# Longer key turns in a planner's prices, a plan searched again under random delays, and weight fetches that wait for copied columns

## The chip, the cores and the metric

One core of a Trainium2 chip. The metric is the device time of one execution in microseconds (us); lower is better. The kernel before took 822.94 us in the median of three runs (822.06 to 825.85).

## The reference, cut to what matters

```
q, k, v: (4, 8, 1152, 64)   w_in: (512, 2048)   w_out: (2048, 512)
q_pool = mean of pairs of rows of q                    # 576 queries per head
scores = q_pool @ k.T / 8;  attn = softmax(scores)     # 576 x 1152 per head
x = (attn @ v), heads side by side                     # 2304 tokens x 512
h = x @ w_in;  g = log(1 + exp(h));  out = g @ w_out   # 2304 x 2048, 2304 x 512
```

Inputs are float32. The kernel splits most operands into a high and a low float16 part and adds three float16 products for each float32 one.

## The kernel before, in words

**Work.** The attention is 16 units, each one batch and two heads. A unit loads its keys and queries (`raw`), measures and splits them (`kcat`, `qcat`, `qlow`), and has the parts transposed by DMA: keys at L819 (`kT <- kcat`), queries at L847 (`qA <- qcat`) and L857. Unit 0 is turned on TensorE instead; unit 1's low query rows are too. Then come the row maxima (`maxima`), scores, exponentials, the product with `v`, and the division by the row sums. The feed-forward layer runs on blocks of tokens. Six blocks are plain (`feed_forward`). The last 1024 tokens go through `seven` in four steps n = 0 to 3 of 256 tokens: a 2 x 2 scheme with seven products in place of eight, first with `w_in` (`product`, in two halves q = 0 and 1, results in buffers `p` and `g`), then with `w_out` (`down`, results in `acc`). It needs sums of weight blocks, which `terms` computes earlier and leaves in DRAM as `td`.

**Fetching the sums.** `fetch_sums(1, ...)` (L1615) brings six pieces of 512 KB for `w_out` into the buffers of `kT`, `kB` and `v`, which are free after the last attention unit. `fetch_first(1, ...)` (L1671) brings two more over a part of `w2`. In the plan each of the six has one of the products of step 0 ahead of it, and the last two have the first products of `down`. These are entries in the planner's list of dependencies and no more: in the program the DMA waits only for what its data need, which is that the buffer is free.

**Order.** All work is a list of tasks, each with ways to run it (engine, price in ns), dependencies, a priority and buffers that it takes and gives back. `Sched.run` (L142) simulates the engines with these prices and writes the instructions of each engine in the order in which the simulation starts them. That order is fixed in the program: each engine, and SP, whose queue issues all DMAs, works in order and waits at each instruction for what its data need. A DMA's price is a pair: time on SP's queue, and time on the wire. Two tables steer it, by kind of task and index: `NUDGE` adds to priorities, and `LEAN` adds to the price of an engine where there is a choice.

The lines that the change touches: L734 (first key load), L819 (key turn), L1417 and L1426 (fetches), L1507 (`held`, the four buffers of one half), L1555 (price of softplus), L1615 (deps of the six fetches), L1617 and L1667 to L1675 (order around `down`).

Of the kernel before, what the change touches and what calls it, by code (L numbers as in the profile page):

```python
# [21 lines left out]
    "prep": [3, 5.75, -3.75, -1.5, -55.75, 25.25, 2, 13.25, 3, -6.5, -78.25, -6.75, -19.25, 0, -13.75, 0],  # L22
    "value": [-1.25, 0.25, 4.75, -3.5, -3.75, 0, 0, -38, -4.25, 0.25, 8.5, 3.25, -12.25, 11.5, 0, 13.25],
    "most": [0, 0, 1.25, 10.25, 8.75, -108.25, 0.5, 0.25, 10, -10.75, -8.25, -2, 3.25, 21, 0.75, 3.75],
    "shift": [-5.75, -8.25, -7.75, -0.25, -13.75, -43.5, 7, 7.5, -72.75, -18.75, -104.5, 2.5, -29.75, -1.5,
        0, 1.25],
    "attend": [-11.75, -4, -2.5, 11.5, -6.75, 0, -14, 0.5, -2, -6, -3.5, 6.25, 11, -45.25, 2.25, 0],
    "product": [1.75, 3.5, -31, 120.75, 50.25, -20.5, 10.5, 3.75, 1, 22, -51, 0, 17.5, 19.75, -10.75, 24.75],
    "close": [0, -4.5, -5.75, 0, 31.5, 23, -18, 0, -49.5, -3.75, -58.75, 5, -17.75, 0.5, -3.25, 0],
    "win": [0, -24.5, -5.75, -9.75, 1.75, 2, -3.75, -3],  # L30
    "wout": [-15, -15.25, 5.75, -10.75, -12.25, 28.75, 12, -11.25, -87.25, -24.25, 1, 4.75, 0, -5.25, 2.25,
        -63.25],
    "wparts": [47.75, 0, 38.75, 3.25, 0, -7, -4.25, 0.75, 6.25, -20.5, 0, 0, -0, -40.75, 0, 0],
    "split": [-2.5, 36.75, -3.5, -25.75, 8.5, 5.5, 2.5, 38.5],
    "up": [-5, 1.5, 0.75, 8.5, 0, -0.75, -20.75, -3.25],
    "down": [-9.5, 7.25, 4.25, 15, 0.5, 0, 17.75, -6.75],
    "terms": [1.5, 11.5, 2.5, 12.25, -13.25, 9.75, 0.75, 0.75, -37, 16.25, -6.5, 8.75, -1.5, -9.5, 9, 14],
    "vsplit": [1.75, 0, 16.5, 11],
    "vup": [23.75, 35.75, 28.5, -6, -22.75, -1, -4.25, 0],
    "vdown": [52.25, 1.5, 9.75, -3.75],  # L40
# [4 lines left out]
        "prep": [-50, 150, 0, -100, -0, -600, 4600, 150, 0, 200, -600, -400, -800, -350, 1350, -50],  # L45
        "value": [-250, -550, 250, 1350, 700, -1500, 0, 1200, -250, 350, 500, -750, -300, 2550, -1300, 0],
        "most": [1250, 0, -850, -750, -100, -350, 0, 1000, 0, 50, -950, -500, -950, -200, 0, -350],
        "shift": [0, -50, -50, -1200, 0, -0, 350, 900, -50, -1700, 3300, -1050, 650, 0, 450, 1200],
        "attend": [-250, 0, -1000, 0, -2650, -700, -50, 0, 0, -850, 4250, 2950, 0, 0, -250, 350],
        "product": [-250, 0, -950, -1050, 7600, 0, 450, -0, -50, -5050, -1250, -1400, 850, 250, -7500, 900],  # L50
        "close": [0, 0, 0, 1000, 4500, -6050, 3100, -50, -800, 750, -150, -4100, -1700, 1600, -200, -3200],
        "win": [150, 1600, -250, -200, -1800, 0, 1150, -100],
        "wout": [50, 0, -4350, 350, -50, 2150, -1600, 150, 750, 1400, -750, -450, 200, -2250, 0, -150],
        "wparts": [4100, -500, -100, -200, -1100, 1300, 900, -3000, 500, 200, -1800, 0, 200, 450, -650, 1200],
        "split": [-100, 0, 300, 1050, -5350, 0, 0, -1300],
        "up": [1400, 200, 1250, 600, -550, 1350, -950, 50],
        "down": [-1300, 0, 450, 400, -1150, 1200, -50, -300],
        "terms": [-50, -50, 1000, -350, 1750, -200, 0, -250, 400, -250, -200, 100, 600, -250, 1050, 0],
        "vsplit": [-200, -350, 50, 1800],
        "vup": [0, 2150, 0, 950, 0, -200, -500, 150],  # L60
        "vdown": [500, 950, -400, 50],
    },
    "ACT": {
        "prep": [0, 50, 0, 7650, -3300, 1050, -800, -2350, 450, -800, 3650, -500, -300, 250, -400, -5500],
        "value": [1250, -3550, 300, -1950, 350, -900, -350, 300, 950, -2450, 0, -1150, 0, 200, -450, 0],
        "most": [1250, -3150, 250, -1150, 0, 0, 300, 50, 1550, 0, 100, -100, 0, 850, -250, 550],
        "shift": [-50, -300, 3850, 0, 5650, -450, 250, -100, 1650, -6250, -2350, 300, 1850, -1350, -600, 0],
        "attend": [3000, 1100, 850, 0, 0, -250, 900, -1100, -400, 0, -1350, -0, -850, -1350, 350, 1600],
        "product": [550, -1000, -800, 700, 4400, -300, -1550, -200, -1650, -600, 0, -0, 100, 1200, 0, 1550],
        "close": [-200, 100, -2200, 1400, 1700, 550, 700, 0, -250, 5100, 1500, 0, 550, -300, 4500, -400],  # L70
        "win": [-3850, -2100, -1300, 0, -6100, -350, 0, -4950],
        "wout": [-200, 0, 0, 0, 1700, 0, -600, -300, 100, 250, 50, 1250, 1500, 1450, -4100, -250],
        "wparts": [-650, -1500, 2700, 850, -200, -4350, -2250, 250, 350, 1550, -2700, -1350, 400, -1900,
            -300, 600],
        "split": [2000, -6050, 0, -3400, -950, -750, -750, 450],
        "up": [200, -50, -3500, 0, 400, 0, -750, 550],
        "down": [-3900, -2450, 0, -550, -1800, -150, 650, -700],
        "terms": [150, -800, -1700, -650, 950, 7200, 200, 100, -1400, 3950, 1550, 0, 500, -4650, 0, -1250],
        "vsplit": [-2700, 5400, 0, -600],
        "vup": [-50, 200, -1400, -1350, 250, 0, -1500, 250],  # L80
        "vdown": [0, -1050, 1150, -900],
# [174 lines left out]
def act(n, psum=0, ap=0):  # L256
    return n * 0.833 + (168.0 if psum else 200.0) + 92.0 * ap
# [11 lines left out]
def tile_attention_softplus_ffn(  # L269
# [9 lines left out]
    nc = tc.nc  # L279
# [181 lines left out]
    def load(fn, queue, wire, deps, prio, take):  # L461
        return task([("DMA", queue + 95.0, fn, wire)], deps, prio, take=take)
# [242 lines left out]
    def prepare(u):  # L705
# [15 lines left out]
        def low():  # L721
# [12 lines left out]
            400.0, 2340., units[u - 1].raw_free if u > 2 else [units[0].kB_done] if u == 2 else [], prio - 6.0, [r])  # L734
# [725 lines left out]
    v_x_free, fives = [], [[], []]  # L1460
# [4 lines left out]
    def seven(n):  # L1465
# [36 lines left out]
        split_done = {}  # L1502
        for q in range(2):
# [3 lines left out]
            held = [Hold(ring, 4) for _ in range(4)]  # L1507
# [38 lines left out]
            def soft(o, i, m, deps, p, take=(), give=()):  # L1546
# [8 lines left out]
                return task([("ACT", 4 * act(128 * m, m == 1, m > 1), fn, "softplus")], deps + exps[NU - 1][-5:] + [f1], p,  # L1555
# [33 lines left out]
            g12 = soft(lambda Q=Q: Q(1), lambda Q=Q: Q(1), 1, [c12], at["P3"] + 1)  # L1589
            prio += 7.5  # L1590
# [26 lines left out]
        o1, o2 = Hold(acc_r), Hold(acc_r)  # L1617
# [56 lines left out]
        c1 = scaled(at(o2, 0), lambda: region("P1"), [ps["P1"]], prio + 2, [o2, o1], [pairs[0]])  # L1674
        u2 = plus(at(o1, 1), "P6", at(o2, 0), [ps["P6"], c1])  # L1675
# [84 lines left out]
```

## Time and profile before

| | |
|---|---|
| median of 3 runs | 822.94 us (822.06 to 825.85) |
| the profiled execution | 822.63 us |
| its span, first to last instruction | 820.8 us |
| TensorE busy | 779.7 us (95%) |
| VectorE, ScalarE, GpSimd busy | 680.9, 556.6, 227.4 us |
| mean granted TensorE clock | 0.995 |

PE is TensorE's matmuls, PEld its weight loads, DVE VectorE, ACT ScalarE, POOL GpSimd, SPq the queue of SyncE that issues the DMAs. L819 is line 819 of the kernel before. A row of the windows gives a stretch from the span's start, its length, the busy time of each engine with its instructions, the granted clock, the DMA engines' busy share and GB/s. The profiled execution is 1.8 us longer than its span and 0.3 us below the median.

### The profile page before, as it was taken

The numbers are of one execution on the slowest core, as the hardware profiler recorded it, in microseconds if no ns is written. First come the engines' busy times: TensorE is split into PE (matmuls) and PEld (weight loads), VectorE is DVE, ScalarE is ACT, GpSimd is POOL, SyncE is SP. The second block draws the span as 40 slices with busy tenths as digits, with TensorE's granted clock in tenths as the row PEclk, the third lists the DMA queues.
The fourth block names the chain that finished last, engine by engine and source line by source line (L and its number), as shares of the span: only waits on it lengthen the run. The fifth ranks groups of instructions, "written<-read, shape, count | busy, mean of one in ns | idle before, by whom it ended". The sixth has DMA issues, their size and how long they took to land.

```text
span 820.8 us, 29645 instructions
## 1 busy us (share of the span) xinstructions
PE 779.7 (95%) x12626; PEld 610.0 (74%) x12626; DVE 680.9 (83%) x1475; ACT 556.6 (68%) x968; POOL 227.4 (28%) x213
## 2 busy tenths in 40 slices
PE   4899999999999999989999999999999799999997
PEld 2556656679765976767976688775677799999995
DVE  7978999899979979878999997987573499889862
ACT  6999899898966567678766676867772457333521
POOL 1000001200443223548459862021722110012100
PEclk9999999999999999999999999999999999999999
DMA  8768969968055475652745354465253600000230
GB/s 272 208 157 219 211 183 218 166 181 226 17 115 159 72 145 139 170 86 81 163 126 104 101 116 125 132 126 76 64 167 72 220 4 4 29 30 3 64 96 15
DMA packets 152400, 99.75 MB, mean 122 GB/s; under 512 B 95180, under 2 KB 132044, under 8 KB 152268
## 3 DMA queue, kind: packets, MB, share of 16 engines
q1 hardware_dynamic: 152268, 97.86, 47.8%
q8 instruction: 99, 1.62, 0.9%
q14 instruction: 33, 0.27, 0.1%
HBM read 60.29 MB, written 15.28 MB: 92 GB/s over the span
## 4 chain that ended last, share of the span: by engine, by line
PE 67%; DVE 16%; DMA 4%; issue 4%; ACT 4%; SPq 2%; POOL 2%; DVEq 0%; ACTq 0%; POOLq 0%
PE s L380 28%; PE m L380 23%; PE pv L1128 13%; DVE g L918 2%; DMA qA<-qcat 1%; PE pv L1144 1%; ACT p L1117 1%; DMA raw<-in_q_dram 1%; DMA raw<-in_k_dram 1%; POOL acc L457 1%; PE m L1199 1%; DVE g L1543 1%; PE pv L380 1%; DVE g L457 1%; DVE raw L372 1%
## 5 line engine op out<-in xcount | busy, mean ns | idle before, releaser
L1117 ACT ACTIVATE p<-s,cols 128x512 f32<-128x512 f32 (+1 forms) x288 | 210.2, 742 | 50.5 <-PE s L380 33.7
L1128 PE MATMUL pv<-p,v 128*64 128x320 f32 (+1 forms) x1152 | 188.2, 414 | 0.9 <-DVE rinv L369 0.9
L380 PE MATMUL s<-qA,kT 128*64 128x320 f16 (+1 forms) x1152 | 158.6, 288 | 4.9 <-ACT p L1117 4.5
L380 PE MATMUL s<-qB,kB 66*64 66x320 f16 (+1 forms) x1152 | 159.1, 288 | 0.0
L457 POOL TENSOR_TENSOR acc<-acc,p 128x512 f32<-128x512 f32 (+1 forms) x76 | 116.4, 1531 | 73.9 <-ACT p L1117 58.0
L380 PEld LDWEIGHTS <-w1h 128*64 128x64 f16 x2560 | 114.6, 110 | 5.9 <-issue 3.4
L918 DVE CUSTOM_DVE_ANT_0 g<-m,g 128x512 f32<-128x512 f32 x142 | 96.2, 682 | 25.5 <-ACT g L914 13.5
L380 PE MATMUL m<-w,gh 128*64 128x512 f16 (+1 forms) x808 | 108.0, 349 | 0.7 <-DVE acc L372 0.6
L380 PEld LDWEIGHTS <-kT 128*64 128x64 f16 x1152 | 80.4, 111 | 31.2 <-issue 11.9
L1128 PEld LDWEIGHTS pv<-p,v 128*64 128x64 f32 x1152 | 78.6, 137 | 29.9 <-issue 11.1
L380 PE MATMUL s<-xo,w1h 128*64 128x256 f16 (+1 forms) x1792 | 100.3, 250 | 0.2 <-DVE xo L372 0.2
L914 ACT ACTIVATE g<-m 128x512 f32<-128x512 f32 x142 | 83.8, 598 | 20.4 <-PE m L380 19.5
L380 PEld LDWEIGHTS <-kB 66*64 66x64 f16 x1152 | 75.6, 110 | 19.1 <-issue 5.2
L380 PEld LDWEIGHTS <-qA 128*64 128x64 f16 x1040 | 62.1, 110 | 34.3 <-issue 12.9
L380 PEld LDWEIGHTS <-gh 128*64 128x64 f16 x944 | 59.7, 110 | 22.0 <-issue 1.6
L380 PE MATMUL m<-kT,qA 128*64 128x512 f16 (+2 forms) x588 | 72.2, 301 | 3.3 <-DVE nm L918 1.9
L457 DVE TENSOR_TENSOR acc<-acc,p 128x512 f32<-128x512 f32 (+1 forms) x92 | 71.4, 776 | 4.0 <-ACT p L1117 3.3
L380 PE MATMUL m<-w,gl 128*64 128x512 f16 (+1 forms) x456 | 72.1, 340 | 0.6 <-DVE acc L372 0.6
L380 PEld LDWEIGHTS <-w1l 128*64 128x64 f16 x1280 | 64.7, 110 | 3.6 <-issue 3.6
L380 PE MATMUL m<-kD,qA 128*64 128x512 f16 x284 | 57.7, 386 | 6.7 <-DMA qA<-qcat 4.9
L380 PE MATMUL s<-xo,w1l 128*64 128x256 f16 (+1 forms) x896 | 63.4, 250 | 0.2 <-issue 0.2
L1362 ACT ACTIVATE g<-s,blk 128x512 f32<-128x512 f32 (+1 forms) x48 | 29.4, 616 | 48.4 <-PE s L380 44.1
(279 smaller groups left out, 1412.3 us busy)
## 6 DMA issues: line engine op xcount, KB each, us to landing
raw<-in_k_dram SPq DMA_DIRECT2D x16, 576.0 KB
v<-in_v_dram SPq DMA_DIRECT2D x16, 576.0 KB
raw<-in_q_dram SPq DMA_DIRECT2D x64, 128.0 KB
raw<-in_moe_w_out_dram SPq DMA_DIRECT2D x16, 512.0 KB
td<-to SPq DMA_DIRECT2D x32, 256.0 KB
kB<-kT SPq DMA_DIRECT2D x32, 144.0 KB
gl<-in_moe_w_in_dram SPq DMA_DIRECT2D x4, 1024.0 KB
gh<-in_moe_w_in_dram SPq DMA_DIRECT2D x4, 1024.0 KB
```

Source lines behind the costliest of these rows:

```text
L372: nc.vector.scalar_tensor_tensor(out=out_, in0=in0, scalar=s, in1=in1, op0=op0, op1=op1)
L380: nc.tensor.matmul(out=out_[c:e], lhsT=lhsT[:, c:e], rhs=rhs, start=start, stop=stop, tile_position=(0, at + c))
L457: e.tensor_tensor(out=o, in0=a, in1=b, op=op)
L914: r = task([("ACT", act(512, 1), lambda: nc.scalar.activation(out=rest.item, in_=more.item, func=ACTF.Relu))], [y], prio, take=[rest], giv ...
L918: parts.append(task([("DVE", dve(512), lambda: nc.vector.tensor_tensor_reduce(out=rest.item, in0=most.item, in1=rest.item, scale=1.0, scal ...
L1117: nc.scalar.activation(out=pt.item[:, :, 0:n], in_=s.item[:, :, 0:n], func=ACTF.Exp, scale=x.sc)
L1128: nc.tensor.matmul(out=pv.item[h * 64:(h + 1) * 64, 0:n], lhsT=x.v.item[:, h, kt], rhs=pt.item[:, h, 0:n], start=(kt == 0), stop=(kt == KT ...
L1144: nc.tensor.matmul(out=pv.item[g:g + 32, 512 - n // 2:512], lhsT=ones[:, 0:32], rhs=pt.item[:, h, a * n // 2:(a + 1) * n // 2], start=Fals ...
L1199: nc.tensor.matmul(out=ps.item[g:g + 32, 512 - n // 2:512], lhsT=ones[:, 0:32], rhs=acc.item[:, h, a * n // 2:(a + 1) * n // 2], start=Tru ...
L1362: x = task([("ACT", act(N, 1, 1), lambda: nc.scalar.activation(out=gs.item[:, 0:N], in_=ps.item[:, 0, 0:N], func=ACTF.Softplus, scale=ih[: ...
L1543: return task([("DVE", dve(512), lambda: nc.vector.tensor_tensor(out=o(), in0=bank_(), in1=i(), op=ALU.add))], deps, p, give=list(give))
```

## The change

- Both tables, `NUDGE` and `LEAN`, hold other numbers throughout, so the order on every engine's queue is another.
- A key turn (L819) is priced at 2750 ns on the queue and 1700 on the wire, before 2095 and 1150. The first key load is priced at 1150 ns, before 400 + 95 as the others (the 95 is added to both). A softplus of four pieces is priced at 1190 or 1650 ns, before 1098 or 2021.
- In step 0 of `seven` GpSimd copies one column of a result into the first column of each buffer that a fetch will overwrite. The fetch then has to wait in the program too: the six for the results u3, c21, c12 of half 0 and then of half 1, the two others for c1 and u2 of `down`. `held`, `o1` and `o2` are given back after these copies as well.
- c1 and u2 of `down` are listed before its third product, and the first product of one step's `down` follows the last of the step before in the plan.

The core of the diff, with the tables left out:

```diff
@@ prepare
-            400.0, 2340., units[u - 1].raw_free if u > 2 else ...
+            400.0 if u else 1150.0, 2340., units[u - 1].raw_free if u > 2 else ...
...
-            x.k_done = [task([("DMA", 2095.0, lambda: nc.sync.dma_start_transpose(
-                out=x.kT.item, in_=cat.item.rearrange("p t d -> p (t d)")), 1150.0, 1700.0)], parts, prio,
+            x.k_done = [task([("DMA", 2750.0, lambda: nc.sync.dma_start_transpose(
+                out=x.kT.item, in_=cat.item.rearrange("p t d -> p (t d)")), 1700.0, 1700.0)], parts, prio,
@@ fetch_sums(w, homes, deps, prio, gates=None)
             h = Hold(homes[2 * (t - 1) + hl])
+            first, take = deps[2 * (t - 1) + hl], [h]
+            if gates:
+                y, i, held = gates[2 * (t - 1) + hl]
+                first, take = [task([("POOL", 150.0, lambda h=h, i=i: nc.gpsimd.tensor_copy(flat(h)[:, 0:1], i()), "port")],
+                                    first + [y], prio, take=take, give=held)], []
@@ fetch_first(w, deps, prio, gate=None)
+            first = deps[hl]
+            if gate:
+                first = [task([("POOL", 150.0, lambda hl=hl: nc.gpsimd.tensor_copy(late["part"](w, hl)[:, 0, 0:1], gate[hl][1]()), "port")],
+                              first + [gate[hl][0], saved[w, hl]], prio, give=[gate[hl][2]])]
@@ seven
-            held = [Hold(ring, 4) for _ in range(4)]
+            held = [Hold(ring, 7 if n == 0 else 4) for _ in range(4)]
...
-                return task([("ACT", 4 * act(128 * m, m == 1, m > 1), fn, "softplus")], ...
+                return task([("ACT", 1190.0 if m == 1 else 1650.0, fn, "softplus")], ...
...
+            if n == 0:
+                for y, i in ((u3, 3), (c21, 2), (c12, 1)):
+                    gates.append((y, lambda i=i, Q=Q: Q(i)[:, 0:1], held))
...
-            fetch_sums(1, [kT_r] * 2 + [kB_r] * 2 + [v_r] * 2, [late["ended"] + [v_x_free[i]] for i in (5, 6, 8, 9, 11, 12)], when)
+            fetch_sums(1, [kT_r] * 2 + [kB_r] * 2 + [v_r] * 2, [late["ended"]] * 6, when, gates)
...
+            if name == "P2":
+                c1 = scaled(at(o2, 0), lambda: region("P1"), [ps["P1"]], prio + 2, [o2, o1], [pairs[0]])
+                u2 = plus(at(o1, 1), "P6", at(o2, 0), [ps["P6"], c1])
             if n == 0 and name == "P5":
-                fetch_first(1, [downs + [ps["P1"]], downs + [ps["P6"]]], prio + 5.0)
+                fetch_first(1, [downs] * 2, prio + 5.0, ((c1, lambda: wide(o2, 0)[:, 0:1], o2), (u2, lambda: wide(o1, 1)[:, 0:1], o1)))
-            ps[name] = down(name, [ps[DOWN[i - 1]]] if i % 2 else [], [] if i % 2 else [pairs[i // 2]])
+            ps[name] = down(name, [ps[DOWN[i - 1]]] if i % 2 else last_down[-1:], [] if i % 2 else [pairs[i // 2]])
+        last_down[:] = [ps["P3"]]
```

## Rows read from the trace of the kernel before

**Rows 1.** Busy time on the page, and its row of TensorE's code loads (packets, MB, share).

```profile
PE 779.7 (95%) x12626; PEld 610.0 (74%) x12626; DVE 680.9 (83%) x1475; ACT 556.6 (68%) x968; POOL 227.4 (28%) x213
q8 instruction: 99, 1.62, 0.9%
```

**Rows 2.** Windows: start, stages of the span, end.

```profile
0.00:20.00 20.00, 8.33 (x96) 5.12 (x96) 15.21 (x32) 13.13 (x23) 2.90 (x9) 1.00 0.83 268
20.00:180.00 160.00, 151.12 (x2073) 98.53 (x2075) 144.06 (x381) 144.99 (x251) 13.48 (x20) 1.00 0.80 198
180.00:640.00 460.00, 450.49 (x6023) 342.42 (x6019) 386.00 (x826) 324.58 (x535) 193.60 (x166) 0.99 0.49 116
640.00:660.00 20.00, 15.64 (x554) 15.34 (x551) 11.12 (x18) 8.42 (x21) 2.31 (x3) 1.00 0.63 213
660.00:800.00 140.00, 138.01 (x3622) 136.77 (x3618) 120.22 (x211) 62.42 (x134) 15.14 (x15) 1.00 0.12 33
```

**Rows 3.** Waits of PE: total us, times, longest.

```profile
PE m L380 <- ACT kcat L547: 6.4, 1, 6.4
PE m L380 <- DMA qA<-qcat: 4.9, 2, 2.6
PE s L380 <- ACT p L1117: 4.5, 9, 1.4
PE m L380 <- issue: 4.4, 2, 3.1
```

**Rows 4.** Windows around those waits for issue.

```profile
643.60:646.20 2.60, 2.43 (x87) 2.29 (x82) 2.34 (x5) 1.47 (x5) 0.74 (x2) 1.00 1.03 413
646.10:647.20 1.10, 0.00 (x0) 0.00 (x0) 0.98 (x2) 0.00 (x0) 0.00 (x0) 1.00 1.00 406
647.28:654.14 6.86, 3.76 (x128) 3.60 (x127) 2.67 (x4) 0.92 (x3) 0.00 (x0) 1.00 0.82 243
```

**Rows 5.** Timeline of PE there (start, length, idle before and releaser).

```profile
647.29 0.33 PE L380 MATMUL m<-xo,w1h 128*64 128x128 f16 x5 [1.27 <-issue]
654.15 0.24 PE L380 MATMUL m<-xo,w1l 128*64 128x128 f16 x1 [3.10 <-issue]
```

**Rows 6.** Timeline of SP's queue: first and last fetches of `w_out` sums.

```profile
638.62 0.98 SPq L1422 DMA_DIRECT2D kB<-td  x1
641.08 1.10 SPq L1422 DMA_DIRECT2D v<-td  x2
642.22 5.05 SPq L1399 DMA_DIRECT2D w<-td  x2
```

**Rows 7.** Chain of waits, near 364 and 568 us.

```profile
360.66 2.92 SPq L819
363.64 4.98 DMA qA<-qcat
568.40 7.22 DMA qA<-qcat
```

**Rows 8.** Windows at those two places.

```profile
366.00:368.00 2.00, 0.36 (x8) 0.09 (x2) 1.36 (x1) 0.84 (x2) 1.08 (x1) 1.00 1.54 107
368.00:374.00 6.00, 5.34 (x40) 3.22 (x42) 2.10 (x6) 3.91 (x8) 3.06 (x5) 0.72 0.77 209
572.00:576.00 4.00, 0.97 (x9) 0.34 (x7) 0.83 (x3) 0.27 (x1) 0.26 (x2) 1.00 1.14 128
576.00:582.00 6.00, 6.00 (x60) 4.22 (x58) 2.54 (x8) 4.22 (x8) 4.49 (x5) 0.72 0.55 156
```

**Rows 9.** Key turns on SP's queue (min/median/max ns, first and last start).

```profile
L819 SPq DMA_TRANSPOSE kT<-kcat x15: 2374/2924/3652, 27.9 to 565.7; - x15
```

**Rows 10.** Timelines: results and first users of fetches, POOL's smallest operation.

```profile
650.45 0.69 DVE L1543 TENSOR_TENSOR p<-s,p 128x512 f32<-128x512 f32 x1 [3.34 <-PE s L380]
670.99 0.68 DVE L1543 TENSOR_TENSOR g<-m,g 128x512 f32<-128x512 f32 x1
674.04 1.50 PE L380 MATMUL m<-kT,gl 128*64 128x256 f16 x24
691.32 1.50 PE L380 MATMUL m<-v,gh 128*64 128x256 f16 x24
659.18 0.48 POOL L428 TENSOR_SCALAR xo<-xT,blk 128x256 f16<-128x256 f32 x1 [14.79 <-PE s L380]
665.55 0.33 PE L380 MATMUL s<-xo,w1h 128*64 128x128 f16 x4
```

More of the change, by code (lines that the diff above doesn't have):

```diff
@@ L21 @@
 NUDGE = {
[L22 to L40, printed above, removed]
+    "prep": [-8, 1.75, -7.75, -55.25, -67.5, 21.5, 3.25, 24.5, -2.5, -3.5, -132.75, -6, -26, 13.25, -5.25,
+        0.5],
+    "value": [7.5, 5.5, 2.25, 8, -9.5, 0.75, 6.75, -49, 0.75, -22.25, -6.25, -3.75, -36, 23.75, -45.5, 11.75],
@@ new lines @@
+    "most": [-3.75, 0.75, 1.75, 22.5, 0.5, -170.75, 0, -7.5, -1, -20.75, -56.5, 0.25, -4.25, -5.75, -3.5,
+        -0.75],
+    "shift": [-20.75, -42.25, -37.5, -2, -0, -134.5, -2.25, -5.75, -218.5, -94.25, 0, 5.75, 6.75, -44.75, -8,
+        25.5],
+    "attend": [-10.75, -4.5, 0, 2.25, 0.5, 1, -14.5, 0.75, 1, -22, 0, -10.5, -0.5, -10, 0, 8.75],
+    "product": [-1.25, 6, -10.75, 126.75, 83.25, -37.25, 10.75, 76, 1.25, 24.5, 0, -10, 21, 0.75, 23, 1.5],
+    "close": [1.25, -4, 2.25, -5.25, 48.5, 24.5, -17.25, 4.25, 5.5, -39.25, -42.25, 0, 10, 12, 23.25, 18.75],
@@ new lines @@
+    "win": [-1.25, -126.25, -9.75, -14.5, -0.5, 13.75, -12, 24],
+    "wout": [-7.5, 57, -4, 0, 0.75, 8, 5, 7.75, 0, 26.25, -0, -0.25, 2.5, 1, 25.5, -43.75],
+    "wparts": [24.75, -11, 0, 18.25, -11.75, 0, 16.75, 0, -23, 0, 2, -5.75, -62, -12, 14.5, 0],
+    "split": [-34.75, 32.5, -6, 17.5, -14.25, 58.75, -22.5, 12.25],
+    "up": [2.75, -0.75, -0.5, 0, 16.75, -15.25, 27, -15.25],
+    "down": [-16.5, 96.5, -3.5, 35.75, 20.5, 0, -12.5, -6],
+    "terms": [-0.75, 5.25, 5.5, -2.75, 0.5, 9.75, 8.5, 6.75, -21.5, 4, -30, -61, 1, 8, -7.75, -12],
@@ L41 @@
+    "vsplit": [-25, 1.5, -0.75, 9.25],
+    "vup": [0, -4, -5, 0, -24.75, 0.75, -3, 27.5],
+    "vdown": [5.25, 23, 34, 82.5],
 }
@@ L44 @@
     "POOL": {
[L45 to L61, printed above, removed]
+        "prep": [-150, 850, -500, -550, 6600, 0, 0, 0, 5950, 0, -200, 0, 3400, 650, 0, -600],
+        "value": [-50, 2050, 1700, 1050, 150, -200, -750, -350, -2850, 200, 1900, 700, 200, 0, -600, 2200],
@@ new lines @@
+        "most": [800, 550, -1650, 3650, -1450, 50, -550, 150, 100, -750, -650, 300, -1100, 1650, -100, 950],
+        "shift": [550, 400, -1550, 1650, -4850, -150, -1000, 0, 50, -4950, 50, 100, -50, 0, 1000, -750],
+        "attend": [0, 300, 1150, 0, 550, 1800, -450, 50, 0, 1400, 400, -1000, 1350, -700, 0, -0],
+        "product": [350, 0, 450, 0, 5450, 100, 0, 300, -5650, -3800, 50, 0, 600, 0, -1850, 0],
+        "close": [2700, 0, 0, 4050, -1650, -7000, 1250, 0, -2800, -5450, -1200, -4300, -3000, -6700, 900, -0],
@@ new lines @@
+        "win": [-1150, 400, -1500, -200, 700, 750, -150, -1500],
+        "wout": [150, -650, -1600, -400, 1350, 950, -400, -750, 0, -1050, -300, -1250, 650, 1350, 1750, -400],
+        "wparts": [2500, -50, 1000, -0, -5100, -150, -50, -4650, 0, 350, -500, 100, 2050, -650, 1750, 1500],
+        "split": [-6500, 4050, 2650, -1150, 900, 400, -900, -3500],
+        "up": [400, 100, 900, -750, -1250, 100, 4350, -1300],
+        "down": [0, -1650, 400, 750, -2450, 1050, 50, 150],
+        "terms": [1650, 50, 550, -400, 0, 0, -150, 250, 0, 0, 900, 0, -850, 600, 1250, 850],
@@ L62 @@
+        "vsplit": [-0, 1150, -300, -150],
+        "vup": [-500, 2250, -250, -2400, -900, 250, -300, -900],
+        "vdown": [-1100, -100, 150, 1800],
     },
     "ACT": {
[L64 to L81, printed above, removed]
+        "prep": [0, -250, -800, 8500, -8700, 950, 200, -2000, 2200, -2400, 8350, 650, -4400, 850, 0, -1000],
@@ new lines @@
+        "value": [-3750, 300, -800, 0, 0, -1650, 1200, -600, -1500, 1950, 2250, 1000, -3800, 0, 0, -1100],
+        "most": [1250, 1700, 600, 450, -450, -5500, 50, -2200, 2900, 0, -300, 7400, -450, -150, 1050, 0],
+        "shift": [0, -2850, 3000, 650, 0, 0, -150, 3700, -200, -0, -350, 0, 350, -1900, 900, 0],
+        "attend": [1000, -4550, -700, 100, 0, 0, -100, -1550, 1300, 1300, 1500, 0, 1650, -750, 400, -350],
+        "product": [-2700, 1300, -50, -0, 50, 0, 150, -1100, 300, 250, 1650, -2150, -50, 550, 2150, -2550],
@@ new lines @@
+        "close": [0, 400, -8650, 10400, 6400, 50, 4200, 350, -950, 1400, -850, -1400, -2100, 2750, -1350,
+            1750],
+        "win": [-3200, -2050, -550, 150, 800, 0, 1350, -9350],
+        "wout": [0, 450, -150, 1950, 0, -350, 150, -400, -2200, 0, -5100, 750, -100, -100, 200, 2800],
+        "wparts": [-850, -3250, -1000, 0, -550, -6350, 0, 0, -3650, 2200, -50, -150, 450, -3050, -450, 550],
+        "split": [-500, -350, 1250, 0, 350, 250, 0, 400],
+        "up": [0, -100, 1400, -3600, -400, -300, 100, 1650],
@@ L82 @@
+        "down": [0, 100, 3150, 0, 2850, -150, 1650, 250],
+        "terms": [300, -1700, -550, -950, 0, -1550, 550, 400, 200, 10650, -4850, -150, -6250, -2200, 4750,
+            1150],
+        "vsplit": [-650, 0, 0, 600],
+        "vup": [-850, -1950, -1300, -1200, -850, 0, -550, 1900],
+        "vdown": [0, -1550, 1650, -250],
     },
@@ L733, in prepare @@
             in_=k[b, 2 * p:2 * p + 2].rearrange("h (p t) d -> p h t d", t=KT)),
-            400.0, 2340., units[u - 1].raw_free if u > 2 else [units[0].kB_done] if u == 2 else [], prio - 6.0, [r])
+            400.0 if u else 1150.0, 2340., units[u - 1].raw_free if u > 2 else [units[0].kB_done] if u == 2 else [], prio - 6.0, [r])
         qr, qc = Hold(raw_r, 2), Hold(qcat_r)
@@ L1415, in spaced, with fetch_sums @@
         return [[tasks[i * len(tasks) // n]] for i in range(n)]
-    def fetch_sums(w, homes, deps, prio):
+    def fetch_sums(w, homes, deps, prio, gates=None):
         flat = late["flat"]
@@ L1421, in fetch_sums, with fetch_first @@
                 h = Hold(homes[2 * (t - 1) + hl])
+                first, take = deps[2 * (t - 1) + hl], [h]
[3 more added lines that the diff above has]
+                                        first + [y], prio, take=take, give=held)], []
                 x = load(lambda h=h, w=w, t=t, hl=hl: nc.sync.dma_start(out=flat(h), in_=td[w][t][:, hl]),
-                         390.0, 2000.0, deps[2 * (t - 1) + hl] + term_done[w], prio, [h])
+                         390.0, 2000.0, first + term_done[w], prio, take)
                 late[w, t, hl] = (x, lambda h=h: flat(h))
-    def fetch_first(w, deps, prio):
+    def fetch_first(w, deps, prio, gate=None):
         for hl in range(2):
@@ L1429, in fetch @@
                 late["moved"](late["part"](w, hl), td[w][0][:, hl], w, False)
-            x = load(fetch, 390.0 * (2 - w), 2000.0, deps[hl] + term_done[w] + [saved[w, hl]], prio, [])
+            first = deps[hl]
+            if gate:
+                first = [task([("POOL", 150.0, lambda hl=hl: nc.gpsimd.tensor_copy(late["part"](w, hl)[:, 0, 0:1], gate[hl][1]()), "port")],
+                              first + [gate[hl][0], saved[w, hl]], prio, give=[gate[hl][2]])]
+            x = load(fetch, 390.0 * (2 - w), 2000.0, first + term_done[w] + [saved[w, hl]], prio, [])
             late[w, 0, hl] = (x, None)
@@ L1459, in tile_attention_softplus_ffn @@
     HL = ((0, 0), (0, 1), (1, 0))
-    v_x_free, fives = [], [[], []]
+    v_x_free, fives, last_down = [], [[], []], []
     def flat2(t):
@@ L1502, in seven @@
         split_done = {}
+        gates = []
         for q in range(2):
@@ L1553, in fn @@
                         nc.scalar.activation(out=a, in_=c, func=ACTF.Softplus, scale=ih[:, 4 * q + jj:4 * q + jj + 1])
-                return task([("ACT", 4 * act(128 * m, m == 1, m > 1), fn, "softplus")], deps + exps[NU - 1][-5:] + [f1], p,
+                return task([("ACT", 1190.0 if m == 1 else 1650.0, fn, "softplus")], deps + exps[NU - 1][-5:] + [f1], p,
                             take=list(take), give=list(give))
@@ L1614, in seven @@
             mark("vsplit", 1)
-            fetch_sums(1, [kT_r] * 2 + [kB_r] * 2 + [v_r] * 2, [late["ended"] + [v_x_free[i]] for i in (5, 6, 8, 9, 11, 12)], when)
+            fetch_sums(1, [kT_r] * 2 + [kB_r] * 2 + [v_r] * 2, [late["ended"]] * 6, when, gates)
         mark("vdown", n)
-        o1, o2 = Hold(acc_r), Hold(acc_r)
+        o1, o2 = Hold(acc_r, 2 if n == 0 else 1), Hold(acc_r, 2 if n == 0 else 1)
         prio = when + 14.0
@@ L1668, in seven @@
         for i, name in enumerate(DOWN):
+            if name == "P2":
+                c1 = scaled(at(o2, 0), lambda: region("P1"), [ps["P1"]], prio + 2, [o2, o1], [pairs[0]])
+                u2 = plus(at(o1, 1), "P6", at(o2, 0), [ps["P6"], c1])
             if n == 0 and name == "P5":
                 mark("vsplit", 1)
-                fetch_first(1, [downs + [ps["P1"]], downs + [ps["P6"]]], prio + 5.0)
+                fetch_first(1, [downs] * 2, prio + 5.0, ((c1, lambda: wide(o2, 0)[:, 0:1], o2), (u2, lambda: wide(o1, 1)[:, 0:1], o1)))
                 mark("vdown", n)
-            ps[name] = down(name, [ps[DOWN[i - 1]]] if i % 2 else [], [] if i % 2 else [pairs[i // 2]])
-        c1 = scaled(at(o2, 0), lambda: region("P1"), [ps["P1"]], prio + 2, [o2, o1], [pairs[0]])
-        u2 = plus(at(o1, 1), "P6", at(o2, 0), [ps["P6"], c1])
+            ps[name] = down(name, [ps[DOWN[i - 1]]] if i % 2 else last_down[-1:], [] if i % 2 else [pairs[i // 2]])
+        last_down[:] = [ps["P3"]]
         c11 = plus(at(o1, 0), "P2", at(o2, 0), [ps["P2"], c1])
```

## The prediction

> **What bounds the kernel now.** I read the page's busy times first: TensorE is busy 779.7 of 820.8 us [rows 1]. What can be won without changing its work is its 41 us of idle time and whatever its clock loses. So the second view is the windows, by stages, for where it idles [rows 2]: 11.7 us before 20 us, 8.9 in the next 160, where VectorE and ScalarE are both busy for 144 to 145 of 160 us, 9.5 in the 460 us from 180, 4.4 in only 20 us from 640, 2.0 in the 140 us after that, and the rest at the end. The third is the waits of PE [rows 3]. Two entries there are long, late in the span and single: 4.4 us in two waits for "issue", which is time in which PE waits for nothing that the profile shows, and 4.9 us in two waits for a query transpose. The reader is to see that the change speaks to these two and that the largest wait, 6.4 us at the start, is the first unit's own chain, of which it alters only the price of one load.
>
> **The wait for issue.** Rows 4 show the DMA engines full at 406 to 413 GB/s when PE stops for the first time. What fills them is on SP's queue: from 638.6 us the six fetches and the two others leave one behind the other, the last two taking 5.05 us to issue because nothing moves ahead of them [rows 6]. Eight pieces of 512 KB are 4.2 MB, at 410 GB/s some 10.2 us. They leave together since the program lets them go as soon as the buffers are free, whatever the plan says. Why should PE care, when it needs none of them for 30 us [rows 10]? Between its two stops [rows 5] it ran 128 matmuls and 127 or 128 weight loads [rows 4], that is 256 instructions; and the page counts 99 code loads of 1.62 MB together [rows 1], 16.4 KB each, for 2 x 12626 = 25252 instructions, 255 to a load. PE therefore stops where one load's worth of code ends. I read this as code that comes late because its transfers share the full DMA engines.
>
> The Trainium skill speaks against this: "Runtime: NRT & Kernel Launch", section "Instruction fetch mechanics", says that the sequencer fetches the next block of code over its own DMA queue while it runs the present one, and that crossing a block is mostly hidden. The trace agrees on the block (256 instructions between stops) and not on the hiding (1.27 and 3.10 us [rows 5]). By the rule the fetches would not be the cause and spreading them would give nothing; that is a rival below.
>
> **The change part by part.**
>
> *The gated fetches.* Removed: the burst, and with it 1.27 + 3.10 = 4.4 us of PE. Each fetch now waits for a result. In the trace of before these results lie from 651.1 us (u3 of half 0, 650.45 + 0.69) to 671.7 (c12 of half 1) [rows 10], so six fetches of 1.3 us each (512 KB at 410 GB/s) are spread over 20 us, and the two of `down` come later still. A single fetch holds the DMA engines for less than the 3.6 us in which PE works through one load of code (256 instructions in 3.76 us [rows 4]), so I expect no stop from one. What is late next? The first product that reads the `kT` fetches starts at 674.0, 22 us or more after their gates, and the one that reads the `v` fetches at 691.3, 19.6 us after the last gate [rows 10]. If one more stop came in place of two, it would be 1.3 to 3.1 us. After 660 us VectorE is busy for 120 of 140 us [rows 2], and during the stop it idled too (11.1 busy of 20), so it can take the earlier start. I count the whole 4.4.
>
> *The copies.* Eight copies of one column on GpSimd. No row shows one. From below they are nothing, as GpSimd is busy for 2.3 us of the 20 from 640 and 15.1 of the 140 after [rows 2]; they remove no work, so they can't gain by themselves. From above each is the smallest operation shown there, 0.48 us [rows 10], 3.8 us together on an idle engine. I take nothing, nearest to what an idle engine charges. What a copy does is wait: behind it on GpSimd stands a split of the next step's tokens (`xo`, 659.18), and behind each gated fetch on SP's queue the next fetch and later the output stores. The stores have 100 us to go; the split does not, and makes the price of a mishap: placed behind the copy that waits for c12 of half 1, it would move from 659.2 to 671.7, and the products at 665.55 [rows 10] with it, by up to 12.5 us less what other products fill. The planner knows this dependency, so I leave it in the upper bound.
>
> *The key turns.* The trace has 2374 to 3652 ns on the queue, 2924 in the middle [rows 9]; the plan counted 2095, and 2750 after. Per turn the plan moves what follows by 655 ns on the queue and 550 on the wire, 1.2 us together. Twice this hits PE: at 360.66 and 565.7 a key turn stands ahead of a query turn on the queue, and PE waits 2.3 and 2.6 us for the query turn [rows 3, 7]. Behind each stands a stretch of lower clock: the granted clock is 0.72 over 368 to 374 and again over 576 to 582, after PE was busy for 0.36 of 2 and 0.97 of 4 us [rows 8]; 0.28 x 6 = 1.7 us each. So the two stops cost 4.9 + 3.4 = 8.3 us. The new prices show the planner 1.2 of the 2.3 to 2.6 us of each, about half. From both sides: nothing, if the new order only moves the stop, and 8.3, if the order puts the query turn first. I take half, 4.1.
>
> *The new order.* Everything else on the queues moves, at prices that are the old ones. PE's idle time from 20 to 640 us is 8.9 + 9.5 = 18.4 us, 13.5 without the two stops. Half of that, 6.7 us, is as much as I would credit to another order; the other side is new stops at (4.9 + 3.4) / 2 = 4.15 us each. A search under random delays should prefer orders with slack ahead of the DMAs, which speaks for fewer such stops, and pay for it in nominal time. I take nothing. The new softplus prices (1190 for 1098, 1650 for 2021) change no instruction by themselves. The order between steps of `down` and the later return of `held`, `o1` and `o2` cost nothing while PE has products at hand; without that cover one product of 1.3 us.
>
> Sum on the profiled execution: 822.63 - 4.4 - 4.1 = 814.1; the median is 0.3 above that execution, so 814.4 us.
>
> **The rivals.**
>
> *Only the fetches count.* The burst goes and the new order is worth what the old one was: 822.9 - 4.4 = 818.5 us. For it: the old tables were fitted as finely, and 13.5 us of idle lie in more than twenty small waits. Against: two waits of a kind whose price was wrong.
>
> *The fetches were not the cause.* PE stops at the same block ends whatever the DMA engines do. Then only the order counts: 822.9 - 4.1 = 818.8, up to 822.9 if that gives nothing too. For it: no row shows the code's own transfers waiting. Against: from 660 to 800 us PE runs 7240 instructions, 28 loads of code, with the DMA engines 12% busy, for 2.0 us of idle in all [rows 2]. This is the case that the rule of the Trainium skill above stands for.
>
> *Slower: more stops behind the transposes.* The turns stay as long as they are; the plan can only shift them, and a query or key turn that lands after its first user costs 4.15 us with its clock. Fifteen units are turned by DMA [rows 9], two of them make PE pay now. With four the time is 822.9 - 4.4 + 2 x 4.15 = 826.8; from five on it is slower, 831.0. For it: DMA engines are 49% busy from 180 to 640 us and the queue is strictly in order, and random delays in a simulation are not those of the chip. Against: the prices are now nearer to the trace's.
>
> *A better order still.* Half of the other idle time goes too: 814.4 - 6.7 = 807.7 us.
>
> **How the numbers follow.** The forecast 0.45, with its own range 810 to 818.5; only the fetches 0.18, half of it on either side of the bound; not the cause 0.10, no change; more stops 0.15, of which 0.11 slower and 0.04 no change; a better order 0.12. With 0.5% (4.1 us, 818.8 to 827.1), about what a measurement of this kernel can tell from no change: faster 0.45 + 0.12 + 0.09 = 0.66, same 0.09 + 0.10 + 0.04 = 0.23, slower 0.11. The range 806 to 827 leaves out the slower case and the far end of the better order, together some 0.16.
>
> **What would show it.** The fetches: the DMA row at 640 to 660 us spread over 20 us or more, no wait for issue of over 1 us there, and PE busy 19 of 20 us. If the wait for issue stays with the DMA engines idle, that step is wrong. The turns: PE's waits for `qA` under 2.5 us in all and no window at a clock of 0.72; if they stand at other units in like size, the order gave nothing. The copies: no wait of PE for `xo` over 1 us. PE's idle time from 20 to 640 us is to be 14 us or less. A median over 818.8 us makes the forecast wrong.

## The result, and the profile after

The changed kernel takes 815.53 us in the median (813.67 to 815.60), the kernel before 823.83 beside it: ratio 0.9874, 95% interval 0.9839 to 0.9908. Another set of runs gave 813.58 against 823.39 us, ratio 0.986 (0.9832 to 0.9888). The forecast was 814.4 us, faster. Both terms of the sum came out near their size. For the fetches the reason held; for the key turns it did not, and that their size met the forecast is luck, as the last part of the account shows.

Busy time on the page after, against [rows 1]. PE's work is the same (12626 matmuls); its idle time within the span is 813.9 - 778.3 = 35.6 us, before 41.1.

```profile
PE 778.3 (96%) x12626; PEld 617.1 (76%) x12626; DVE 677.2 (83%) x1455; ACT 557.8 (69%) x982; POOL 244.1 (30%) x239
```

Windows of the kernel after, by the stages of [rows 2].

```profile
0.00:20.00 20.00, 9.11 (x88) 5.50 (x90) 14.36 (x30) 12.47 (x22) 2.90 (x9) 1.00 0.82 271
20.00:180.00 160.00, 148.33 (x2022) 95.91 (x2019) 142.23 (x369) 142.05 (x249) 11.09 (x16) 1.00 0.76 192
180.00:640.00 460.00, 453.43 (x6259) 354.05 (x6257) 392.57 (x851) 328.76 (x551) 185.87 (x167) 1.00 0.49 118
640.00:660.00 20.00, 19.85 (x574) 18.41 (x570) 15.50 (x27) 11.08 (x27) 2.15 (x6) 1.00 0.50 162
660.00:800.00 140.00, 138.52 (x3602) 136.60 (x3599) 112.02 (x180) 62.79 (x135) 42.05 (x41) 1.00 0.15 41
```

Idle time of PE, before to after: 11.7 to 10.9 us up to 20 us, 8.9 to 11.7 up to 180, 9.5 to 6.6 up to 640, 4.4 to 0.15 up to 660, 2.0 to 1.5 up to 800. So the stage of the fetches gives 4.2 us, the middle of the attention 2.9, and the first attention units give 2.8 back. The mean granted clock went from 0.995 to 0.999.

The waits of PE after, against [rows 3]: the one for query transposes is gone and those for issue are down from 4.4 + 0.2 to 1.8 us; waits for exponentials and row maxima (`ACT p`, `ACT g`) grew from 4.5 + 0.5 to 6.3 + 3.3.

```profile
PE s L382 <- ACT p L1119: 6.3, 12, 1.4
PE m L382 <- ACT kcat L549: 6.3, 1, 6.3
PE m L382 <- ACT g L916: 3.3, 5, 1.4
PE s L382 <- issue: 1.8, 3, 1.0
```

SP's queue after, the fetches of [rows 6]. They now leave one or two at a time: the six from 639.7 to 652.2 us, over 12.5 us where the prediction had 20, and the two others at 665.6 and 676.0.

```profile
639.69 3.01 SPq L1429 DMA_DIRECT2D kT<-td  x2
646.73 3.00 SPq L1429 DMA_DIRECT2D kB<-td  x2
650.13 2.40 SPq L1429 DMA_DIRECT2D v<-td  x2
665.57 0.37 SPq L1401 DMA_DIRECT2D w<-td  x1
676.03 0.38 SPq L1401 DMA_DIRECT2D w<-td  x1
```

The copies, on GpSimd's timeline after: 0.19 to 0.32 us for the six (two of them shown), 0.76 and 0.64 for the two others (one shown).

```profile
639.47 0.19 POOL L1427 CAST kT<-p 128x1 f16<-128x1 f32 x1 [9.37 <-DVE p L1555]
651.87 0.32 POOL L1427 CAST v<-g 128x1 f16<-128x1 f32 x1 [1.77 <-DVE g L1555]
664.78 0.76 POOL L1440 CAST w<-acc 128x1 f16<-128x1 f32 x1 [11.51 <-ACT acc L1666]
```

### The profile page after: what moved, and what is told of

Same layout as the page of the kernel before. It is cut to its first block, busy times and chain, and to the rows that moved or that the text cites. A ratio compares the mean times of both kernels' runs of the same rounds, so it can differ in the third digit from the quotient of the medians.

```text
span 813.9 us, 29672 instructions
## 1 busy us (share of the span) xinstructions
PE 778.3 (96%) x12626; PEld 617.1 (76%) x12626; DVE 677.2 (83%) x1455; ACT 557.8 (69%) x982; POOL 244.1 (30%) x239
## 4 chain that ended last, share of the span: by engine, by line
PE 72%; DVE 11%; ACT 7%; DMA 4%; issue 4%; SPq 1%; POOL 1%; ACTq 0%; DVEq 0%; POOLq 0%
PE m L382 28%; PE s L382 27%; PE pv L1130 12%; ACT p L1119 2%; DVE acc L459 2%; DVE g L920 2%; PE pv L1146 2%; DMA raw<-in_moe_w_out_dram 1%; PE pv L382 1%; DMA td<-to 1%; ACT g L916 1%; PE m L1201 1%; DVE kcat L374 1%; DVE w L374 1%; DMA few<-rinv 1%
## 5 line engine op out<-in xcount | busy, mean ns | idle before, releaser
L382 PEld LDWEIGHTS <-w1h 128*64 128x64 f16 x2560 | 117.7, 110 | 4.5 <-issue 2.3
L459 POOL TENSOR_TENSOR acc<-acc,p 128x512 f32<-128x512 f32 (+1 forms) x68 | 100.9, 1484 | 49.8 <-ACT p L1119 16.1
L382 PE MATMUL m<-w,gh 128*64 128x512 f16 (+1 forms) x832 | 110.3, 346 | 0.0
L382 PEld LDWEIGHTS <-qA 128*64 128x64 f16 x1048 | 66.4, 111 | 37.1 <-issue 20.9
L382 PEld LDWEIGHTS <-kB 66*64 66x64 f16 x1152 | 77.4, 110 | 19.3 <-issue 5.4
L382 PE MATMUL m<-kT,qA 128*64 128x512 f16 (+2 forms) x628 | 79.1, 300 | 6.6 <-ACT g L916 2.8
L459 DVE TENSOR_TENSOR acc<-acc,p 128x512 f32<-128x512 f32 (+1 forms) x100 | 77.2, 772 | 4.9 <-ACT p L1119 3.8
L382 PEld LDWEIGHTS <-gh 128*64 128x64 f16 x992 | 65.4, 110 | 19.6 <-issue 0.3
L382 PE MATMUL m<-w,gl 128*64 128x512 f16 (+1 forms) x440 | 75.9, 342 | 0.0
L382 PEld LDWEIGHTS <-w1l 128*64 128x64 f16 x1280 | 67.3, 110 | 1.3 <-issue 1.2
```

What stands on the lines that cost most here:

```text
L382: nc.tensor.matmul(out=out_[c:e], lhsT=lhsT[:, c:e], rhs=rhs, start=start, stop=stop, tile_position=(0, at + c))
L459: e.tensor_tensor(out=o, in0=a, in1=b, op=op)
```

## The experiments

### The fetch part alone

The kernel before with the fetch part of the change; its tables, the prices of the key turn, the first load and softplus are those of before, so every queue's order up to the last attention unit is the same.

```diff
-    NUDGE, LEAN of the changed kernel
+    NUDGE, LEAN of before
-    key turn 2750.0, 1700.0; first key load 1150.0; softplus 1190.0, 1650.0
+    key turn 2095.0, 1150.0; first key load 400.0;  softplus as computed before
```

> The kernel before with the fetch part alone (copied columns, later return of held, o1 and o2, order around down); tables and all prices of before, so the order up to about 630 us is that of before. Theory (the burst of fetches delays TensorE's code): the two waits for issue go, PE waits for issue under 1 us between 630 and 665 us, the two waits for query transposes (4.9 us) stay, time 4 to 4.5 us under before, ratio 0.995. Rival (the stops do not come from the fetches): the waits for issue stay at 4.4 us and the time is that of before, ratio 1.000.

Measured 819.50 against 824.17 us, ratio 0.9943 (0.9921 to 0.9965). Its profiled execution was the quickest of its 12 runs (815.33, the others up to 823.52), so its waits are read here and not its span: for issue 0.2 us in one wait, for query transposes as before. The granted clock fell behind only the second of these two here.

```profile
PE m L380 <- DMA qA<-qcat: 4.8, 2, 2.6
PE s L380 <- issue: 0.2, 1, 0.2
```

What follows: the fetch part is worth 4.7 us, and the waits that it was to remove are the ones that went. That they go is not certain in every execution. With the old order five of the six fetches still leave within 7.1 us (647.2 to 654.2 us here). In the second profiled execution of this same kernel (the run beside the changed kernel, below) the same five left from 651.6 to 658.7 us, and PE stopped for issue for 1.58 us; its window, then its timeline:

```profile
656.00:658.00 2.00, 2.00 (x79) 2.00 (x75) 1.97 (x4) 1.18 (x3) 0.64 (x1) 1.00 0.91 367
```

```profile
660.00 0.35 PE L380 MATMUL m<-xo,w1h 128*64 128x128 f16 x5 [1.58 <-issue]
```

### The copies elsewhere, in the changed kernel

Order and instructions of all queues as in the changed kernel; only the target of the eight copies differs, so nothing waits for them.

```diff
-    nc.gpsimd.tensor_copy(flat(h)[:, 0:1], i())
+    nc.gpsimd.tensor_copy(spare[:, e:e + 1], i())
```

> The changed kernel with the same order on every queue, but the eight copies write into a spare tile, so no fetch waits for them. Theory: the fetches leave together again when the last attention unit has ended, DMA engines full for about 10 us, waits for issue rise from 1.8 to between 4.5 and 6.5 us, time 3 to 4.5 us over the changed kernel, 818.5 to 820. Rival (the new order alone does it): 815.5 us, waits for issue as in the changed kernel.

Measured 817.73 us, ratio 0.9914 (0.9889 to 0.994); 2.2 us over the changed kernel's first median, 4.2 over its second, which were taken at other times; its interval overlaps that of the first and not that of the second. The six fetches left within 3.4 us of each other (632.5 to 635.9 us), but the two into `w2` did not join them (660.5 and 680.5), so the burst was 3.1 MB and not 4.2. PE stopped once for 2.0 us where the DMA engines were full, and ran at a lower clock after it; its windows, then its timeline:

```profile
638.00:642.00 4.00, 2.00 (x66) 1.84 (x62) 0.60 (x2) 0.75 (x2) 0.00 (x0) 0.96 1.02 404
642.00:646.00 4.00, 4.00 (x97) 4.00 (x92) 1.34 (x2) 0.00 (x0) 0.19 (x1) 0.62 0.33 129
```

```profile
641.11 4.10 PE L382 MATMUL s<-xo,raw 128*64 128x128 f16 x81 [2.00 <-issue]
```

The waits for issue came to 3.7 us, under the 4.5 expected; 2.0 of them are this stop and 1.46 one at 792 us, where the changed kernel has 1.03. The direction is the theory's, the size smaller, as the burst was.

### Half the burst, in the kernel before

This kernel leaves out four of the eight fetches; only its time and its stops are read.

```diff
-    nc.sync.dma_start(out=flat(h), in_=td[w][t][:, hl])
+    None if w and t == 1 else nc.sync.dma_start(out=flat(h), in_=td[w][t][:, hl])
...
-    late["moved"](late["part"](w, hl), td[w][0][:, hl], w, False)
+    None if w else late["moved"](late["part"](w, hl), td[w][0][:, hl], w, False)
```

> The kernel before, order unchanged, with four of the eight fetches left out (the two into kT, whose old contents are multiplied in their place, and the two into w2): 2.1 MB, some 5 us of full DMA engines. Theory: only what goes past one load of code (3.6 us of work) stops PE, so one stop of 0 to 1.5 us in place of 4.4 us, time 3 to 4.4 us under before, ratio 0.995 to 0.9965. Rival: stops at ends of code loads whatever the DMA engines do, ratio 1.000.

Measured 819.08 us, ratio 0.9937 (0.9912 to 0.9962), 5.1 us under the kernel before: more than the 3 to 4.4 of the theory, whose ratio (0.995 to 0.9965) lies partly in the interval, and far from the rival's 1.000. The stops are as the theory had them: of 1.27 + 3.10 us [rows 5] the first is left with 1.28 us, the second with 0.25. The first on PE's timeline:

```profile
646.11 0.33 PE L380 MATMUL m<-xo,w1h 128*64 128x128 f16 x5 [1.28 <-issue]
```

### A burst added to the changed kernel, at two places

```diff
+    if n == 1 and t == 2 * cc + 1:      # the other kernel: if n == 0 and t == 2 * cc
+        for e in range(8):
+            nc.sync.dma_start(out=junk[e], in_=td[0][e // 2][:, e % 2])
```

> The changed kernel with a burst of its own added late: eight copies of 512 KB from DRAM to DRAM behind an output store of step 1 of seven (around 710 us), which nothing reads or waits for. Theory: PE stops for issue there, 3 to 6 us more in all, time 3 to 6 us over the changed kernel, 818.5 to 821.5. Rival (code does not share what the fetches fill): 815.5 us and no new wait for issue.

Measured 820.07 us, ratio 0.9947 (0.9928 to 0.9966), 4.5 over the changed kernel's first median, inside what the theory expected, and not by its mechanism. PE ran through 16 us of full DMA engines without a stop; then VectorE stood for 4.8 us, waiting for an output store that was caught in the burst, and PE waited 2.7 us for VectorE. PE's windows, then VectorE's timeline:

```profile
730.00:746.00 16.00, 16.00 (x346) 16.00 (x342) 13.10 (x21) 8.11 (x18) 1.72 (x2) 1.00 0.93 288
```

```profile
747.90 0.43 DVE L459 TENSOR_TENSOR acc<-xT 128x256 f32<-128x256 f32 x1 [4.80 <-DMA out_dram<-acc]
```

The row also says something new: 346 + 342 instructions in 16 us are 2.7 loads of code, one in 6 us, where the stops of before came with one in 3.8 us of work [rows 4]. That suggests that a burst hurts where code is used up fast. The second place has faster products and no store for 40 us:

> The changed kernel with eight copies of 512 KB from DRAM to DRAM behind the stores of step 0 of seven (around 690 us), where no store or fetch follows for 40 us, so that only code can be late. PE runs 26 to 31 matmuls per us there, before the earlier added burst 20. Theory: DMA engines full for 13 us while PE needs a load of code every 4 to 5 us: one to three waits for issue, 2 to 5 us more, 817.5 to 820.5. Rival (code is late only beside fetches into SBUF): no new wait for issue, 815.5.

Measured 818.90 us, ratio 0.9927 (0.9904 to 0.995), 3.4 over the changed kernel's first median. PE stops for 2.0 us towards the end of the burst; the profiled execution was itself a quick one (814.96), so the stop is read here and not the difference of the spans. The windows and the waits from 690 to 710 us:

```profile
700.00:704.00 4.00, 2.08 (x75) 1.92 (x70) 3.05 (x4) 3.68 (x9) 3.84 (x4) 1.00 0.88 291
```

```profile
PE pv L382 <- issue: 2.0, 1, 2.0
```

In the changed kernel the same 4 us are full (4.00 busy, DMA engines 2%). So copies that touch no buffer of PE, and for which nothing waits, stop PE at "issue": that full DMA engines cause such stops is now shown by adding, by halving and by spreading the burst. That it is the code that comes late is read from the code loads themselves, in the last section.

### The prices without the search, and the search without the prices

The changed kernel with the old tables:

> The changed kernel with the old two tables: new prices and the fetch part, no new search. Theory (the prices alone let the planner avoid the late query transposes): waits for query transposes under 2.5 us in all, time 4 us under that of the fetch part alone, 814 to 816.5. Rival (the tables fit one set of prices and the search does the work): another order that nothing has tuned, waits elsewhere of 4 us and more, 818 to 828 us.

The changed kernel with the old turn and load prices:

```diff
-    key turn 2750.0, 1700.0; first key load 1150.0
+    key turn 2095.0, 1150.0; first key load 400.0
```

> The changed kernel with the old price of a key turn (2095 and 1150 ns) and of the first key load, new tables. Theory (the search does the work, at its prices only): another order, 818 to 828 us. Rival (the new tables carry the gain whatever the price): 815.5 us within 2.

Measured 862.35 us, ratio 1.0448 (1.0408 to 1.0489), and 840.90 us, ratio 1.0207 (1.0168 to 1.0246): both far worse than the kernel before, and outside both forecasts, theory and rival. Against the fetch part alone, which the first of the two holds as well, it is 43 us. The right prices with tables that fit the wrong ones still leave waits for query transposes:

```profile
PE m L380 <- DMA qA<-qcat: 4.0, 3, 1.4
```

Neither half of the pair won anything by itself. What the change brings here is a new search at new prices; how much the better price made that search better, these runs can't tell. The new softplus price stood in both kernels and was not run by itself.

### The query turn ahead of the key turn

The fetch part alone, with one edit: in units 10 and 15 two neighbours on SP's queue change places.

```diff
-    ... kT <- kcat (L819), qA <- qcat (L847)
+    ... qA <- qcat (L847), kT <- kcat (L819)      # units 10 and 15
```

> The kernel of the fetch part alone with one edit: in units 10 and 15 the query turn goes ahead of the key turn on SP's queue, all other queues unchanged. Theory (the stop is the key turn ahead of the query turn): the query transposes land some 2.7 us earlier, PE's waits for them fall from 4.8 us to under 1, the windows of half clock behind them go, time 4 to 8 us under that of the fetch part alone, 811.5 to 815.5. Rival (keys are needed as soon): the wait moves to the keys and kD, which come 1.4 us later, time within 2 us of the fetch part alone, 817.5 to 821.5.

Measured 821.62 us, ratio 0.9968 (0.9945 to 0.9991): nothing won, 2.1 us over the fetch part alone, taken at another time (the two intervals overlap). The wait for queries is gone from the list and waits for `kD`, which is made from keys, and for `sh`, which stands behind `kD` on VectorE, are in its place; the clock behind them falls as before (0.72 over 368 to 374 us). PE's waits, VectorE's wait for keys at the second place, then the chain of waits at the two places:

```profile
PE m L1004 <- DVE sh L372: 4.2, 2, 3.8
PE m L380 <- DVE kD L457: 2.8, 2, 2.6
```

```profile
577.03 0.43 DVE L457 TENSOR_TENSOR kD<-kT 128x512 f16<-128x512 f16 x1 [5.03 <-DMA kT<-kcat]
```

```profile
362.16 6.36 DMA kT<-kcat
568.52 8.49 DMA kT<-kcat
```

The rival stands: keys and queries are needed at the same time, and it is not their order that makes PE wait.

### Both parts side by side, and under a disturbance

The changed kernel and the fetch part alone, again, in one set of runs:

> The changed kernel as it is, beside the fetch part alone on the same chip, to size what the new order adds. Forecast from the earlier runs: 815.5 us; ratio to before 0.987 to 0.991, of which the fetch part is 0.995.

> The fetch part alone again, beside the changed kernel on the same chip. Theory (the new order is worth some 4 us of its own): 3 to 6 us over the changed kernel. Rival (all of the gain is the fetch part): within 1.5 us of it.

Measured 813.58 us, ratio 0.986 (0.9832 to 0.9888), and 818.39 us, ratio 0.9921 (0.9895 to 0.9948), with 823.39 before: 5.0 us for the fetch part, 4.8 for the rest, and the two intervals do not overlap. The first ratio is just under the 0.987 to 0.991 forecast.

The same two with 16 copies that nothing reads:

```diff
+    nc.sync.dma_start(out=junk[u], in_=v[b, 2 * p:2 * p + 2])     # ahead of each unit's load of v
```

> The fetch part alone with a copy of 590 KB from DRAM to DRAM put on SP's queue ahead of each unit's load of v, 16 in all, which nothing reads: about 1.5 us of full DMA engines and 0.5 us of queue time each. Theory (an order searched without delays has little slack ahead of its transposes): it loses 6 us or more to its undisturbed form. Rival (slack is alike): it loses as much as the changed kernel does, within 2 us.

> The changed kernel with the same 16 copies at the same places. Theory (an order searched under random delays has slack for them): it loses at most 3 us to its undisturbed form, less than half of what the old order loses. Rival: both lose alike, within 2 us.

Measured 827.41 us (1.0022, 0.9998 to 1.0046) and 822.07 us (0.9972, 0.9949 to 0.9996): 9.0 and 8.5 us lost. The order searched under random delays is no more tolerant of this disturbance than the old one. My theory of its slack falls; that it would be more tolerant of another kind of delay was not tried.

## Why the prediction was right, point by point

- **The gated fetches, 4.4 us.** Right in mechanism, and the time is near: 4.7 and 5.0 us for the part alone. The stops that went from its two profiled executions, 4.4 us and 2.7 us, are less than that; where the rest of its gain lies is not shown. The rule of the Trainium skill that I weighed against it ("Runtime: NRT & Kernel Launch", "Instruction fetch mechanics": the next block of code is fetched while the present one runs, so a crossing is mostly hidden) holds in this case where PE uses a load of code in 6 us and fails beside full DMA engines where it uses one in less than 4. Three short waits for issue stay in the changed kernel (0.56, 1.03 and 0.26 us); the longest, at 787.6 us, stands behind DMA engines that are full from 784 to 786 us (last section). I had set "no wait for issue of over 1 us" for 640 to 660 us, and in the changed kernel it holds there; in the fetch part alone it failed once (1.58 us).
- **One fetch at a time is harmless.** Right where they leave one or two at a time: no stop for issue lies between 630 and 780 us in the changed kernel. Five within 7.1 us, in the fetch part alone, stopped PE in one of two profiled executions.
- **The copies at nothing.** Right; 0.19 to 0.76 us each, on an engine that idles before them.
- **The key turns, 4.1 us.** The sum is right (4.8 us for all that is not the fetch part), the step "the new prices show the planner 1.2 of the 2.3 to 2.6 us of each, about half" failed. The new prices with the old tables gave a kernel 38 us slower than the one before, and another order of the two turns won nothing. In the changed kernel the turns are no quicker (a median of 3303 ns on the queue, 2924 before [rows 9]), and in the two places the turned keys and queries are first used some 9.4 and 7.7 us after the key turn's start, where PE before took them 8.0 and 9.9 us after it. At the second place the new order even has the query turn first (at 567.72, the key turn at 569.11), which won nothing when it was done alone. The difference is what PE does meanwhile. The windows after, from the key turns at 359.54 and 569.11, against [rows 8]:

```profile
359.00:363.00 4.00, 4.00 (x48) 2.93 (x45) 4.00 (x9) 0.79 (x1) 3.84 (x3) 1.00 0.74 122
363.00:367.00 4.00, 4.00 (x57) 2.70 (x54) 2.86 (x6) 3.66 (x8) 2.80 (x4) 1.00 1.13 168
367.00:371.00 4.00, 4.00 (x47) 2.71 (x44) 2.63 (x5) 3.67 (x10) 3.92 (x4) 1.00 0.82 217
569.00:573.00 4.00, 4.00 (x62) 2.71 (x56) 3.21 (x10) 2.02 (x4) 0.85 (x2) 1.00 1.13 208
573.00:577.00 4.00, 4.00 (x59) 3.03 (x57) 2.13 (x5) 2.79 (x5) 3.52 (x5) 1.00 1.14 182
```

  PE is full across both turns: the new order has kept scores and products of the unit before for these microseconds. The whole 8.3 us of the two stops went, not half, clock included: the granted clock is at its full level from 20 to 812 us, where before it stood at half of that in a stretch behind each stop.
- **The new order at nothing.** Not so: it gave back part of those 8.3 us. PE's idle time from 20 to 640 us was to be 14 us or less and is 18.2, 18.4 before. What left the two stops came back in waits of at most 1.4 us each: 1.8 us more for exponentials (`ACT p`), 2.8 more for row maxima (`ACT g`), 0.8 more for `kD`. Behind none of them does the granted clock fall, and so the same idle time costs less: the mean granted clock, 0.995 to 0.999, is worth some 3.3 us of the 820 (an estimate), of which 1.4 appear in PE's busy time. So the forecast 4.1 met the measured 4.8 by luck: too little was credited to the key turns and nothing was charged to the new order, and the two errors work against each other. The 4.8 us I can't place term by term; the profiled executions of the two kernels differ by single microseconds from run to run.
- **The rivals.** "Only the fetches count" (818.5 us) and "not the cause" (818.8) are both ruled out by the pair 813.58 and 818.39. "More stops behind the transposes" did not come about: even the slow kernel with the old tables waits for query transposes for no more than before (4.0 us); what it loses lies in many other waits (TensorE idle for 65 us, before 41) and in the clock (0.980).

## What to carry to other kernels

A dependency that stands only in a planner holds nothing back on the chip: check in the trace that transfers leave when the plan says, and give those that must be spread a real dependency, such as a one-column copy into their target. When an order was searched at one set of prices, the tables and the prices are one object: prices corrected without a new search made a kernel 38 us slower here. A late transfer need not come sooner; work kept back for its time removes the stop and the lower clock behind it.

## What the runs showed of the hardware

TensorE waits for "issue" next to transfers that have nothing to do with it, mostly longer where more is moved at once, and where it uses up code fast:

| kernel | burst | PE's stops for issue there |
|---|---|---|
| before | 4.2 MB into SBUF | 1.27 + 3.10 us |
| copies elsewhere | 3.1 MB into SBUF | 2.00 us |
| half the burst | 2.1 MB into SBUF | 1.28 us |
| burst between stores | 4.2 MB, DRAM to DRAM | 2.0 us |
| burst added, PE at 22 matmuls per us | 4.2 MB, DRAM to DRAM | none |
| fetch part alone, two executions | 2.6 MB into SBUF, in 7.1 us | none; 1.58 us |
| changed kernel, 640 to 676 us | one or two pieces of 0.5 MB at a time | none |
| changed kernel, 782 to 787 us | 1.3 MB: two pieces into SBUF, one output store | 1.03 us |

The trace holds each code load as a packet of 16 KB on the instruction queue [rows 1], and these packets show the step that was argued so far. Full DMA engines did not make these loads slower, they let them start late. In the kernel before, the loads at the two stops took 0.95 and 1.19 us, the median of all 99 is 1.11. From 667 to 774 us, with the DMA engines 5% busy, each load starts within 0.6 us of the moment at which PE begins the block of code ahead of it. Beside the burst the two loads started 2.85 and 4.39 us after that moment; they landed at 646.04 and 652.87 us, and PE went on 1.26 and 1.28 us later [rows 5]. In all these kernels every wait of PE for issue that the profile lists ends 1.2 to 1.5 us after a code load has landed, and the counts of matmuls and weight loads at these places differ by multiples of 256, give or take one. The added burst that did not stop PE made loads late too, by 2.3 to 3.7 us, but there the blocks ahead of them lasted 5 to 10 us. What a late load queues behind, no view shows.

I had not expected that a burst which leaves TensorE alone still reaches it through an output store: VectorE could not reuse an accumulator for 4.8 us. Nor does a stop for issue need the DMA engines to be full while it lasts: they are idle from 788 to 790 us in the changed kernel, in the stop of 1.03 us (787.63 to 788.66), but full from 784 to 786, where the code load for it was due; it started at 786.11, 2.27 us after PE began the block ahead, and landed at 787.19. For the stops of 0.56 us (at 622 us, DMA engines 17% busy over the 2 us before) and 0.26 us (at 792 us) the load was late as well, and why is open.

```profile
784.00:786.00 2.00, 2.00 (x80) 2.00 (x76) 1.93 (x5) 0.79 (x2) 0.00 (x0) 1.00 1.07 298
788.00:790.00 2.00, 1.34 (x49) 1.34 (x50) 0.01 (x1) 0.98 (x2) 0.00 (x0) 1.00 0.01 2
```
